# Dealing MLP groups out by TensorE's time, with their results worked on one phase later, in a fused attention and gMLP kernel

## The chip, the cores and the metric

The kernel runs on one core of a Trainium2 chip, alone. The metric is the time of one execution on the device in microseconds (us); a kernel is judged by the median of several runs. The five engines of the core work through instruction streams of their own, each in program order: TensorE (PE in the profile) does matrix products into PSUM, VectorE (DVE), ScalarE (ACT) and GpSimd (POOL) do elementwise work, and SyncE (SP) issues most DMAs.

## The reference

Eight batches of block-causal attention (8 heads, 576 positions, 64 columns a head), whose output, with the heads side by side, goes through a gated MLP with a mixing product along the positions:

```python
scores = scale * np.matmul(q, k.transpose(0, 1, 3, 2))
scores = np.where(block_i >= block_j, scores, -1000000000.0)      # blocks of 64
attn = softmax(scores)                                             # max, exp, sum
x = np.matmul(attn, v)            # -> (8, 576, 512), heads side by side
h = np.maximum(x @ w_in, 0.0)                                      # 512 -> 1024
u, v = h[..., :512], h[..., 512:]
v_n = (v - mu) / np.sqrt(var + 1e-06)                              # over the 512 columns
v_s = np.einsum('ts,bsd->btd', w_spatial, v_n) + b_spatial[None, :, None]
return (u * v_s) @ w_out                                           # 512 -> 512
```

## The kernel before

All of it is one program that Python writes out step by step; a pool of tiles and semaphores adds the waits, and `own(...)` keeps every instruction at the place on its engine at which it was written. So the order of the Python loop is the order of each engine's stream.

**Steps.** The heads are taken two at a time: 8 batches of 4 pairs, 32 pairs, and a pair is seven steps (`NS = 7`), one for each of the `SLOTS` into which its softmax is cut. Slot 0 is the last 64 queries of both heads, slots 1 and 2 the first 256 queries of the two heads, slots 3 and 4 the next 128, slots 5 and 6 the last 128. At step 0 of a pair TensorE gets the score products of slots 0, 1 and 2 (`scores_last`, L295, and `scores`, L283), at step 3 (`RUN2`) those of slots 3 to 6 and, behind them, the product of the probabilities with v (`av`, L464 and L481) of an earlier pair. Step i runs `exps` of slot i: VectorE subtracts the mask and finds the maximum (L318, L327), ScalarE takes the exponential with its sum (L334). `norm`, one step later, has VectorE invert the sums (L345, L348) and GpSimd multiply (L352). Then the probabilities are transposed, by VectorE and a DMA through the tile `turned` (L408, `move` L422), or in the first batch and the last pair by TensorE (L380).

**Split operands.** From the second batch on, products are made of two parts, a rounded `hi` and the rest `lo`, with three products for one. Each pair's q and k are split by `prep_pair`, which starts at step 4 of the pair before: ScalarE copies both halves of `raw` to `hi` (L244), then GpSimd subtracts four slices into `lo` (L247), two of them written at step 4 and two at step 5. There is one `hi` and one `lo` tile: `hi` can be rewritten only when the current pair's score products of step 3 are done, and the next pair's `scores_last` at step 0 needs the last slice of `lo` in its third product.

**MLP groups.** When a batch's four pairs are through, `moe(b)` makes a queue of 29 groups of matmuls, each into one of four PSUM banks (`ps_m`, shared with `av`): 5 `v_group` (V below; L512, and L522 for the short fifth one), 8 `u_group` (U, L606), 8 `sp_group` (S, L630 to L635) and 8 `out_group` (O, L664). They are dealt out over the 28 steps of the next batch: each step adds `rate` (groups by steps) to `credit`, and one group is written for each whole credit, whatever it takes. A group's result is worked on later: `later(k, phase, f)` has f written k steps on, in that step's phase. `due(0)` comes first in a step, before the scores and the exponentials; `due(1)` behind `exps` and `norm`; `due(2)` and `due(3)` at the end, behind the groups. Of a group written in step n, the first work on its result (ScalarE's relu or copy, L530, L615, L672; VectorE's gate, L639) is written in phase 0 of step n+1, so ahead of the exponentials of that step.

**The first batch.** Its pairs use `raw` as it is and have no groups beside them; the weights are loaded and split meanwhile and during the second batch (`spread(weights, ...)`), on VectorE, ScalarE and GpSimd.

## Time and profile before

| | us |
|---|---|
| runs of the kernel before | 791.61, 807.21, 800.57 (median 800.57) |
| the profiled execution, its time | 797.51 |
| its span, first to last instruction | 795.7 |
| first batch, without split operands | 4.80 to 56.77 |
| pairs beside which weights are still prepared | 56.77 to 203.10 |
| five like batches and one pair more | 203.10 to 683.25 |
| last pair and what is left of the MLP | 683.25 to 795.7 |

The profile is that of one execution. A row of the chain of waits gives a start, a duration and the piece of work; a row of the timeline gives the same and, in square brackets, how long the engine had stood idle before it and what released it. A row of the table of stretches gives the length of a stretch, the busy time of the five engine columns with their numbers of instructions, TensorE's granted clock as a share of full speed, and the share and rate of the DMA engines. PEld is TensorE's weight loading, which runs beside the products. Times count from the span's start. The boundaries of the table above are starts of `scores_last` of a pair.

### The profile page before, as it was taken

The page shows a single profiled execution, that of the slowest core. Times are in us where ns is not written, and L with a number is a line of the kernel's source. Part 1 is how long each engine was busy: PE and PEld are TensorE (multiplying, and loading weights), DVE is VectorE, ACT ScalarE, POOL GpSimd, SP SyncE. Part 2 cuts the span into 40 slices and gives each one's busy share as a digit, 9 for nine tenths or more (in the row PEclk, how much of TensorE's full clock was granted, in tenths as well). Part 3 has the DMA queues.
Part 4 walks back from the last instruction along what each step waited for, and adds up shares of the span by engine and source line. Part 5 has one row for each costly group of instructions (what it writes and reads, how often), then busy time and mean ns, then how long its engine had stood idle before and what let it go on. Part 6 is the DMA issues. An engine that isn't in the chain of part 4 may idle for free.

```text
span 795.7 us, 16364 instructions
## 1 busy us (share of the span) xinstructions
PE 715.7 (90%) x5729; PEld 635.5 (80%) x5729; DVE 465.2 (58%) x1587; ACT 426.4 (54%) x1156; POOL 342.6 (43%) x529
## 2 busy tenths in 40 slices
PE   8876968898988898998988899988988989899998
PEld 5554757787888787887878788887878988799898
DVE  5657877754774557745684557745675456731430
ACT  5775574443663457634763457634664437642542
POOL 4557467642444543344434543355344434341011
PEclk9997877989998999999998999999989889899999
DMA  7322445334444454345444354444544344431001
GB/s 259 123 72 93 128 126 157 88 116 136 124 116 130 127 157 112 105 123 146 130 130 130 101 165 115 113 115 139 152 129 102 97 121 132 98 99 36 26 1 60
DMA packets 42150, 92.05 MB, mean 116 GB/s; under 512 B 9298, under 2 KB 18002, under 8 KB 42068
## 3 DMA queue, kind: packets, MB, share of 16 engines
q1 hardware_dynamic: 32852, 81.56, 37.8%
q10 hardware_dynamic: 9216, 9.44, 3.5%
q8 instruction: 45, 0.74, 0.4%
q14 instruction: 37, 0.30, 0.1%
HBM read 38.18 MB, written 9.44 MB: 60 GB/s over the span
## 4 chain that ended last, share of the span: by engine, by line
PE 66%; POOL 13%; DVE 9%; issue 5%; ACT 4%; DMA 2%; SPq 1%; POOLq 0%; DVEq 0%; ACTq 0%
PE mo L664 10%; PE ms L630 10%; PE mu L606 10%; PE s L283 9%; PE mv L512 9%; POOL lo L247 7%; PE avh L464 6%; POOL p L352 4%; PE s L295 3%; PE avl L464 3%; DVE p L318 2%; PE avh L481 2%; DVE q L408 2%; ACT p L334 1%; PE t L380 1%
## 5 line engine op out<-in xcount | busy, mean ns | idle before, releaser
L334 ACT ACTIVATE p<-p,nmax 128x384 f32<-128x384 f32 (+4 forms) x288 | 167.3, 582 | 207.0 <-DVE nmax L318 97.0
L352 POOL TENSOR_SCALAR p<-p,ssum 128x384 f32<-128x384 f32 (+4 forms) x288 | 161.5, 575 | 197.9 <-DVE ssum L348 166.0
L247 POOL TENSOR_TENSOR lo<-raw,hi 128x288 fp32r<-128x288 f32 x112 | 95.3, 872 | 110.4 <-issue 89.0
L318 DVE CUSTOM_DVE_ANT_0 p<-s,mask 128x128 f32<-128x128 f32 (+3 forms) x256 | 117.3, 481 | 21.0 <-PE t L380 13.9
L606 PE MATMUL mu<-x,wi_hi 128*128 128x288 f32 x512 | 119.9, 316 | 0.0
L408 DVE STREAM_TRANSPOSE q<-p 128x384 f32<-128x384 f32 (+1 forms) x189 | 108.6, 612 | 16.7 <-POOL p L352 8.2
L649 POOL TENSOR_TENSOR gl<-u,gh 128x288 fp32r<-128x288 f32 x64 | 51.7, 809 | 110.5 <-ACT gh L648 110.5
L639 DVE TENSOR_TENSOR u<-ms,u 128x288 f32<-128x288 f32 x64 | 29.2, 456 | 116.2 <-PE ms L635 116.2
L606 PEld LDWEIGHTS mu<-x,wi_hi 128*128 128x128 f32 x512 | 91.9, 204 | 3.7 <-issue 0.9
L512 PE MATMUL mv<-wi_hi,x 128*128 128x512 f32 x256 | 84.5, 397 | 0.0
L630 PE MATMUL ms<-ws_hi,vh 128*128 128x288 f32 x256 | 82.7, 323 | 0.2 <-ACT q L386 0.2
L630 PE MATMUL ms<-ws_lo,vh 128*128 128x288 f32 x256 | 79.6, 311 | 0.0
L630 PE MATMUL ms<-ws_hi,vl 128*128 128x288 f32 x256 | 79.6, 311 | 0.0
L664 PE MATMUL mo<-gh,wo_hi 128*128 128x288 f32 x256 | 77.8, 304 | 0.0
L664 PE MATMUL mo<-gl,wo_hi 128*128 128x288 f32 x256 | 76.8, 300 | 0.0
L664 PE MATMUL mo<-gh,wo_lo 128*128 128x288 f32 x256 | 76.7, 299 | 0.0
L295 PE MATMUL s<-hi,lo 128*128 128x288 f32 x56 | 22.3, 399 | 59.4 <-POOL lo L247 59.4
L606 PE MATMUL mu<-x,wi_lo 128*128 128x288 f32 x256 | 75.4, 314 | 0.0
L295 PEld LDWEIGHTS s<-hi,lo 128*128 128x128 f32 x56 | 12.7, 227 | 64.5 <-POOL lo L247 64.5
L512 PEld LDWEIGHTS mv<-wi_hi,x 128*128 128x128 f32 x256 | 48.4, 189 | 10.8 <-issue 0.6
L630 PEld LDWEIGHTS ms<-ws_hi,vh 128*128 128x128 f32 x256 | 52.4, 205 | 3.0 <-issue 1.3
L334 ACT ACTIVATION_READ_ACCUMULATOR p<-p,nmax 128x1 f32 x288 | 54.3, 189 | 0.0
(118 smaller groups left out, 1620.7 us busy)
## 6 DMA issues: line engine op xcount, KB each, us to landing
turned<-q SPq DMA_DIRECT2D x216, 100.0 KB, 2.2
turned<-q SPq DMA_DIRECT2D x216, 96.0 KB, 2.2
raw<-qk SPq DMA_DIRECT2D x31, 608.0 KB, 4.1
v<-v SPq DMA_DIRECT2D x32, 320.0 KB, 4.3
outT<-o ACTq DMA_DIRECT2D x64, 144.0 KB, 1.8
rwi<-w_in SPq DMA_DIRECT2D x8, 512.0 KB, 4.3
rwo<-w_out SPq DMA_DIRECT2D x4, 512.0 KB, 4.4
rws<-w_spT SPq DMA_DIRECT2D x4, 288.0 KB, 3.1
```

Of the source, the lines that this page charges most:

```text
L247: own(nc.gpsimd.tensor_tensor(out=lo[:, cs], in0=raw[:, cs], in1=hi[:, cs].bitcast(F32), op=ALU.subtract))
L283: own(nc.tensor.matmul(banks[(b, pr, i + hd)][:, o:o + n], a[js, qs], k[js, :n], start=(m == 0), stop=(m == len(parts) - 1),))
L295: own(nc.tensor.matmul(bk[z][:, :HT], a[:, Q8:], k[:, z * HT:(z + 1) * HT], start=(m == 0), stop=(m == len(parts) - 1),))
L318: own(nc.vector.tensor_tensor_reduce(out=pt[:, o:o + n], in0=bk[:, o:o + n], in1=mask[:, 512 - n:], scale=-0.125, scalar=BIG, op0=ALU.add, ...
L334: own(nc.scalar.activation(pt[:, o:o + n], pt[:, o:o + n], AF.Exp, bias=mx, scale=-1.0, accum_out=ssum[:, s0 + r:s0 + r + 1],))
L352: own(nc.gpsimd.tensor_scalar(out=pt[:, o:o + w], in0=pt[:, o:o + w], scalar1=ssum[:, r:r + 1], scalar2=1.0, op0=ALU.mult, op1=ALU.mult,))
L408: own(nc.vector.transpose(to[:, :, o:o + 32 * n].rearrange("p r (c j) -> p c r j", j=32), pt[:, :n * P].rearrange("p (c r j) -> p c r j", ...
L464: own(nc.tensor.matmul(out[js, (t0 - q0) * P:(t1 + 1 - q0) * P].rearrange("p (t a j) -> p a t j", a=4, j=32), vt[:, c, js], src[:, :, o:o ...
L512: own(nc.tensor.matmul(ps, xs[k][:, j, cs], w[:, k, DH:], start=(n == 0), stop=(n == 3 * NC - 1),))
L606: own(nc.tensor.matmul(ps[:, :HT], w[:, k, ds], xs[k][:, j, zs], start=(n == 0), stop=(n == 3 * NC - 1),))
L630: own(nc.tensor.matmul(ps[:, :HT], a[:, ds], w[:, k, zs], start=(n == 0), stop=False))
L664: own(nc.tensor.matmul(ps[:, :HT], w[:, k, es], a[:, k, :], start=(n == 0), stop=(n == 3 * ND - 1),))
```

## The change

Three things are changed.

The queue of groups carries with each group a length in us of TensorE's time (V 2.75, U 1.6, S 1.85, O 1.6), and `PAIR_LENGTHS` has that of the score products of step 0 (1.8), of those of step 3 (1.45) and of `av` (2.95). A step adds `pace`, the batch's whole length over its steps, to `owed`; the score products and `av` take their length off it; groups are written while `owed` is above 0. So the steps with score products get few groups or none and the others get more. In the queue the U group that stood between the fourth and the fifth V group moves behind the fifth.

What is done with a group's result moves from phase 0 to phase 1 of the next step, behind that step's exponentials: the copies, relus and gates. What stood in phase 1 (the rest of x, L443, and the gate's splitting, L648 and L649) moves to phase 2; the tail copy of x (L489) and `begin(b)` move a step on, and the rest of the V groups (L582) moves ahead of the groups of its step.

In the first batch `av` and TensorE's transposes come a step sooner, and the second batch's first pair, the first with split operands, is split from step 2 to step 5 of the pair before it instead of steps 4 and 5.

```diff
-AV_AT, BOOT_AV = 2 * NS + RUN2, NS + 5
+AV_AT, BOOT_AV = 2 * NS + RUN2, NS + 4
+
+PAIR_LENGTHS = (1.8, 1.45, 2.95)
@@ x_evac, av
-        later(1, 0, hi)
-        later(1, 1, lo)
+        later(1, 1, hi)
+        later(1, 2, lo)
...
-        later(1, 2, lambda: own(nc.gpsimd.tensor_scalar(
+        later(2, 1, lambda: own(nc.gpsimd.tensor_scalar(
@@ v_group
-            later(1, 0, evac)
+            later(1, 1, evac)
             later(1, 2, stats)
             later(2, 1, scale)
             later(2, 2, normal)
-            later(3, 2, rest)
+            later(3, 1, rest)
@@ u_group, sp_group, out_group
-            later(1, 0, evac)
+            later(1, 1, evac)
...
-            later(1, 0, gate)
-            later(1, 1, split_g)
+            later(1, 1, gate)
+            later(1, 2, split_g)
...
-            later(1, 0, leave)
+            later(1, 1, leave)
@@ the queue
-        def groups(f, need, *args):
-            return [(need, lambda a=a: f(*a)) for a in args]
+        def groups(f, length, need, *args):
+            return [(need, lambda a=a: f(*a), length) for a in args]
...
-        order = "vvuvuvuvuuuuu" if b else "v" * 5 + "u" * 8
+        order = "vvuvuvvuuuuuu" if b else "v" * 5 + "u" * 8
@@ begin
-        rate = len(queue) / steps if b < B - 1 else 1.0
+        pace = (sum(q[2] for q in queue) + sum(PAIR_LENGTHS) * steps / NS) / steps
@@ the loop over steps
-            if i == RUN2 + 1 and b > 0:
-                spread(prep_pair(b, pr), 6, n, n + 2)
+            if i == (2 if boot else RUN2 + 1) and b > 0:
+                spread(prep_pair(b, pr), 6, n, n + (4 if boot else 2))
...
-                    later(1, 3, lambda b=b: begin(b))
+                    later(2, 1, lambda b=b: begin(b))
...
-        if at(n - 4) and by_pe(at(n - 4)[:2]):
-            for j in TURNS[(i - 4) % NS]:
-                transposes_pe(*at(n - 4)[:2], j)
-        credit = min(credit + rate, 2.0)
-        while credit >= 1.0 and queue and queue[0][0]():
-            queue.pop(0)[1]()
-            credit -= 1.0
+        if at(n - 3) and by_pe(at(n - 3)[:2]):
+            for j in TURNS[(i - 3) % NS]:
+                transposes_pe(*at(n - 3)[:2], j)
+        if here and not boot and i in (0, RUN2):
+            owed -= PAIR_LENGTHS[0] if i == 0 else PAIR_LENGTHS[1]
+        if i == RUN2 and NPAIR + 1 < g < len(pairs):
+            owed -= PAIR_LENGTHS[2]
+        owed = min(owed + pace, 3.0)
+        while owed > 0.0 and queue and queue[0][0]():
+            _, group, length = queue.pop(0)
+            group()
+            owed -= length
```

The first place to look at is TensorE in the fifth batch's first pair (its number is 4, its pair 0; an S group is `ms`, numbered by batch, half and column block). Before, the S group `ms_2_1_1` follows `av`:

```order
L464 MATMUL avl_3_2_4276<-turned_122,v_3_2_3968 64x128 x2
L464 MATMUL avh_3_2_4277<-turned_122,v_3_2_3968 64x128 x14
L481 MATMUL avh_3_2_4277<-turned_122,v_3_2_3968 64x64 x10
L630 MATMUL ms_2_1_1_4324<-ws_hi_114,vh_2_0_3598 128x288
L630 MATMUL ms_2_1_1_4324<-ws_lo_115,vh_2_0_3598 128x288
L630 MATMUL ms_2_1_1_4324<-ws_hi_114,vl_2_0_3599 128x288
```

After the change it ends ahead of the score products of step 3, here those of slots 3 and 4:

```order
L636 MATMUL ms_2_1_1_4251<-ws_a_116,vs_a_118 128x288
L637 MATMUL ms_2_1_1_4251<-ws_b_117,vs_b_119 128x288
L285 MATMUL s_4_0_3_4272<-hi_4_0_4046 128x384
L285 MATMUL s_4_0_4_4273<-hi_4_0_4046 128x384
L285 MATMUL s_4_0_3_4272<-lo_4_0_4047,hi_4_0_4046 128x384
L285 MATMUL s_4_0_4_4273<-lo_4_0_4047,hi_4_0_4046 128x384
```

No group is left at this step. The groups behind `av` and ahead of the next pair's `scores_last` are, for the four kinds of pair from the one with the fourth V group on, V U V' U before and V V' U after; U S S S both times; S O S O before and O S O S after; O O O V V before and O V V after (V' is the short fifth V group).

VectorE's stream at that place keeps its rows: before,

```order
L318 ISA p_4_0_3_4321,nmax_4_0_3_4319<-s_4_0_3_4260,mask_93 128x384
L318 ISA nmax_4_0_3_4319 128x1
L639 TENSOR_TENSOR u_2_3606<-ms_2_1_1_4324,u_2_3606 128x288
L318 ISA p_4_0_4_4348,nmax_4_0_4_4347<-s_4_0_4_4261,mask_93 128x384
L318 ISA nmax_4_0_4_4347 128x1
L443 TENSOR_TENSOR x_3_2_4339<-avl_3_2_4276,x_3_2_4339 128x256
```

and after,

```order
L320 ISA p_4_0_3_4333,nmax_4_0_3_4331<-s_4_0_3_4272,mask_93 128x384
L320 ISA nmax_4_0_3_4331 128x1
L641 TENSOR_TENSOR u_2_3648<-ms_2_1_1_4251,u_2_3648 128x288
L320 ISA p_4_0_4_4347,nmax_4_0_4_4346<-s_4_0_4_4273,mask_93 128x384
L320 ISA nmax_4_0_4_4346 128x1
L445 TENSOR_TENSOR x_3_2_4350<-avl_3_2_4288,x_3_2_4350 128x256
```

The gate of `ms_2_1_1` still stands between the maxima of slots 3 and 4, but the group that it waits for now stands ahead of `av` on TensorE instead of behind it.

The third place is ScalarE in the same batch's pair 2, from the exponential of slot 3 to the copies to `hi`. Before, the relu of the fourth V group (`mv_3_3`) stands ahead of the exponential of slot 4:

```order
L334 ACTIVATE p_4_2_3_4925,ssum_4_2_3_4924<-p_4_2_3_4925,nmax_4_2_3_4923 128x384
L566 ACTIVATE vr_3_2_4814<-vr_3_2_4814,st_3_2_4815 128x512
L574 CAST vh_3_2_4947<-vr_3_2_4814 128x512
L439 CAST x_4_0_4950<-avl_4_0_4880 128x256
L439 CAST x_4_0_4950<-avh_4_0_4881 128x320
L530 ACTIVATE vr_3_3_4932<-mv_3_3_4931 128x512
L334 ACTIVATE p_4_2_4_4960,ssum_4_2_3_4924<-p_4_2_4_4960,nmax_4_2_4_4959 128x384
L244 CAST hi_4_3_4965<-raw_4_3_4736 128x576
L244 CAST hi_4_3_4965<-raw_4_3_4736 128x640
```

and after:

```order
L336 ACTIVATE p_4_2_3_4924,ssum_4_2_3_4923<-p_4_2_3_4924,nmax_4_2_3_4922 128x384
L617 ACTIVATE u_3_4840<-mu_3_0_1_4843 128x288
L568 ACTIVATE vr_3_2_4813<-vr_3_2_4813,st_3_2_4814 128x512
L576 CAST vh_3_2_4932<-vr_3_2_4813 128x512
L336 ACTIVATE p_4_2_4_4940,ssum_4_2_3_4923<-p_4_2_4_4940,nmax_4_2_4_4939 128x384
L441 CAST x_4_0_4944<-avl_4_0_4879 128x256
L441 CAST x_4_0_4944<-avh_4_0_4880 128x320
L246 CAST hi_4_3_4948<-raw_4_3_4736 128x576
L246 CAST hi_4_3_4948<-raw_4_3_4736 128x640
```

The relu of the fourth V group has gone behind the copies to `hi`, and the relu of a U group has come in behind the exponential of slot 3.

More of the change, by code (lines that the diff above doesn't have):

```diff
@@ L673, in leave @@
                 nc.scalar.dma_start(outT[b, es, z * HT:(z + 1) * HT], o)
-            later(1, 0, leave)
-        def groups(f, need, *args):
-            return [(need, lambda a=a: f(*a)) for a in args]
+            later(1, 1, leave)
+        def groups(f, length, need, *args):
+            return [(need, lambda a=a: f(*a), length) for a in args]
         def free():
             return True
-        vs = groups(v_group, free, *((c,) for c in range(FULL + 1)))
-        us = groups(u_group, free, *((z, d) for z in range(2) for d in range(ND)))
-        sps = [groups(sp_group, lambda: ready["v"] > FULL, *((z, d) for d in range(ND)))
+        vs = groups(v_group, 2.75, free, *((c,) for c in range(FULL + 1)))
+        us = groups(u_group, 1.6, free, *((z, d) for z in range(2) for d in range(ND)))
+        sps = [groups(sp_group, 1.85, lambda: ready["v"] > FULL, *((z, d) for d in range(ND)))
                for z in range(2)]
-        outs = [groups(out_group, lambda z=z: ready[z] == ND, *((z, e) for e in range(NO)))
+        outs = [groups(out_group, 1.6, lambda z=z: ready[z] == ND, *((z, e) for e in range(NO)))
                 for z in range(2)]
-        order = "vvuvuvuvuuuuu" if b else "v" * 5 + "u" * 8
+        order = "vvuvuvvuuuuuu" if b else "v" * 5 + "u" * 8
         queue = [(vs if w == "v" else us).pop(0) for w in order]
@@ L751 @@
     queue = []
-    rate = 0.0
-    credit = 0.0
+    pace = 0.0
+    owed = 0.0
     TURNS = ((0,), (), (1, 2), (), (3, 4), (), (5, 6))
@@ L767, in begin @@
     def begin(b):
-        nonlocal rate
+        nonlocal pace
         queue.extend(moe(b))
         steps = NPAIR * NS + (0 if b else AV_AT - BOOT_AV)
-        rate = len(queue) / steps if b < B - 1 else 1.0
+        pace = (sum(q[2] for q in queue) + sum(PAIR_LENGTHS) * steps / NS) / steps
     n = -1
```

## The prediction

> **What bounds the kernel now.** I read the page first, then TensorE's waits, the table of stretches, and the timeline around one wait.
>
> ```profile
> span 795.7 us, 16364 instructions
> ...
> PEclk9997877989998999999998999999989889899999
> ...
> PE 66%; POOL 13%; DVE 9%; issue 5%; ACT 4%; DMA 2%; SPq 1%; POOLq 0%; DVEq 0%; ACTq 0%
> ```
> ```profile
> PE s L295 <- POOL lo L247: 61.5, 26, 4.8
> ```
>
> TensorE is the bound, but the chain leaves it for a quarter of the span, through GpSimd and VectorE, and its clock is below full in most of the 40 slices. One wait dominates: 61.5 us in 26 waits of `scores_last` for the last slice of `lo`. Next the stretches: five batches, cut where the pair with the fourth V group starts, and one pair more; then the stages with weights and at the end.
>
> ```profile
> 203.10:295.45 92.35, 84.71 (x706) 76.61 (x705) 56.84 (x198) 50.12 (x138) 40.72 (x65) 0.94 0.47 126
> 295.45:384.51 89.06, 81.72 (x705) 73.97 (x704) 56.35 (x198) 50.12 (x138) 40.06 (x64) 0.98 0.47 127
> 384.51:476.35 91.84, 84.48 (x705) 76.61 (x704) 56.38 (x198) 50.13 (x138) 40.09 (x64) 0.94 0.47 128
> 476.35:567.10 90.75, 83.23 (x706) 75.43 (x704) 56.13 (x198) 50.00 (x138) 40.07 (x64) 0.96 0.46 125
> 567.10:663.16 96.06, 88.72 (x705) 80.45 (x704) 56.77 (x198) 50.34 (x138) 40.06 (x64) 0.89 0.45 122
> 663.16:683.25 20.09, 20.09 (x167) 17.64 (x166) 16.40 (x61) 14.85 (x39) 6.02 (x11) 1.00 0.42 115
> ```
> ```profile
> 56.77:203.10 146.33, 118.40 (x862) 102.53 (x860) 99.39 (x306) 77.75 (x209) 85.36 (x113) 0.85 0.45 122
> ...
> 683.25:795.70 112.45, 106.60 (x841) 101.03 (x839) 34.83 (x105) 45.73 (x113) 22.85 (x35) 0.97 0.17 48
> ```
>
> A batch takes 92.0 us on average (460.06 over five), with some 7 us of TensorE idle and 0.89 to 0.98 of the clock. The clock is the second loss: behind a wait TensorE often runs at half clock, as here behind the waits that ended at 407.43 and 429.90 us.
>
> ```profile
> 409.20:412.60 3.40, 3.40 (x15) 3.40 (x16) 2.98 (x17) 1.90 (x4) 1.36 (x2) 0.51 0.69 241
> ...
> 430.00:436.60 6.60, 6.60 (x32) 6.10 (x33) 1.09 (x5) 1.19 (x3) 2.73 (x4) 0.50 0.54 173
> ```
>
> Why is `lo` late? The timeline of a pair of the S O S O kind:
>
> ```profile
> 349.19 0.40 PE L283 MATMUL s<-hi,lo 64*128 64x512 f32 x2
> ...
> 352.57 0.43 ACT L439 CAST x<-avh 128x320 fp32r<-128x320 f32 x1 [1.24 <-PE avh L481]
> ...
> 354.60 0.46 DVE L639 TENSOR_TENSOR u<-ms,u 128x288 f32<-128x288 f32 x1 [4.33 <-PE ms L635]
> ...
> 355.63 0.62 ACT L334 ACTIVATE p<-p,nmax 128x384 f32<-128x384 f32 x1 [2.63 <-DVE nmax L318]
> ...
> 356.57 1.30 ACT L244 CAST hi<-raw 128x576 fp32r<-128x576 f32 x2
> ...
> 358.00 1.58 POOL L247 TENSOR_TENSOR lo<-raw,hi 128x288 fp32r<-128x288 f32 x2 [0.44 <-ACT hi L244]
> ...
> 359.55 0.30 POOL L489 TENSOR_SCALAR xs<-x 128x128 fp32r<-128x128 f32 x1
> ...
> 359.83 1.15 POOL L352 TENSOR_SCALAR p<-p,ssum 128x384 f32<-128x384 f32 x2
> ...
> 360.94 1.67 POOL L247 TENSOR_TENSOR lo<-raw,hi 128x288 fp32r<-128x288 f32 x2
> ...
> 362.66 0.40 PE L295 MATMUL s<-hi,lo 128*128 128x288 f32 x1 [2.63 <-POOL lo L247]
> ```
>
> The scores of step 3 end at 349.59 and `av` at 352.55 (2.98). Then TensorE runs an S group, whose gate stands on VectorE ahead of slot 4's maximum: VectorE is idle 4.33 us, ScalarE 2.63 behind it, and `hi`, `lo`, the multiplications and the last `lo` follow in line until 362.61. The whole softmax chain starts when the group behind `av` has ended, 5 us after its scores were there.
>
> **The change part by part.** It adds no instruction. *The groups' results behind the exponentials, and no group at step 3.* Nothing on VectorE or ScalarE now waits for a group behind `av` before `hi` is copied; `av` itself still stands ahead, for x's copies come before `hi`. So from `av`'s end: copy of x 0.43, `hi` 1.30, `lo` 1.58, multiplications 1.15, xs 0.30, `lo` 1.67, sum 6.43 us. What covers it are the groups behind `av` and two products of `scores_last` that need no late `lo` (0.27). Their durations:
>
> ```profile
> 344.71 1.59 PE ms L630 x12
> ...
> 346.57 1.60 PE mo L664 x12
> ...
> 388.13 2.76 PE mv L512 x12
> ...
> 390.89 1.58 PE mu L606 x12
> 392.46 1.42 PE s L283 x12
> ```
>
> S is 1.86 with its two last products, O 1.60, V 2.76, U 1.58, V' 1.9 (8 of V's 12 products). Behind `av` stand after the change U S S S = 7.2, S and O twice = 6.9, O V V = 7.1: more than 6.16 (6.43 less 0.27), by 0.7 to 1.0. These three waits should go, if no engine arrives late. V V' U = 6.2 would just do, but there ScalarE and VectorE are full. Its rows before:
>
> ```profile
> 395.65 0.62 ACT L334 ACTIVATE p<-p,nmax 128x384 f32<-128x384 f32 x1 [1.22 <-POOL p L352]
> 396.27 0.82 ACT L566 ACTIVATE vr<-vr,st 128x512 f32<-128x512 f32 x1
> 397.12 0.62 ACT L574 CAST vh<-vr 128x512 fp32r<-128x512 f32 x1
> ...
> 399.80 0.60 ACT L530 ACTIVATE vr<-mv 128x512 f32<-128x512 f32 x1 [1.45 <-PE mv L512]
> 400.29 0.61 ACT L334 ACTIVATE p<-p,nmax 128x384 f32<-128x384 f32 x1
> 400.89 1.29 ACT L244 CAST hi<-raw 128x576 fp32r<-128x576 f32 x2
> ...
> 405.25 2.13 POOL L247 TENSOR_TENSOR lo<-raw,hi 128x288 fp32r<-128x288 f32 x2
> ...
> 407.43 0.40 PE L295 MATMUL s<-hi,lo 128*128 128x288 f32 x1 [2.40 <-POOL lo L247]
> ```
>
> The exponential of slot 3 starts at 395.65, late by itself. From there, after the change: it 0.62, a relu of U 0.4, 0.82 and 0.55 for the V group, slot 4's 0.61, x 0.35 and 0.43, `hi` 1.29, so 400.7 instead of 402.2; then 1.58, 1.15, 0.30 and 1.7 make 405.5 instead of 407.4. TensorE, its scores done at 393.9, `av` 2.98, groups 6.2 and 0.27, is there at 403.3: a wait of 2.2 stays, for one U has left this pair.
>
> A batch by pairs: 384.51 to 405.5 is 20.7 from the third product of `scores_last` on. The others are TensorE's own work, `scores_last` to `scores` 1.7 and 1.42, `av` 2.98, and groups: U⁴+U S³ 19.5, S³O+S²O² 20.0, O⁴+O V² 19.6. Sum 79.8, and 1.3 for half clock, since one wait in four stays (a stretch of 3.4 us costs 1.7): 81.1 instead of 92.0. Five batches save 54.6, the pair more loses 0.6: **54**. Bounds: 0, if the chain does not shorten, and 70, if the batch is TensorE's own 77.5 at full clock.
>
> *The stage with weights*, 56.77 to 203.10: 27.9 idle (146.33 less 118.40) and 0.15 of the clock, 22. The sooner split works on the first wait:
>
> ```profile
> 60.23 2.12 POOL L247 TENSOR_TENSOR lo<-raw,hi 128x288 fp32r<-128x288 f32 x2
> ...
> 62.39 0.61 PE L295 MATMUL s<-hi,lo 128*128 128x288 f32 x1 [4.84 <-POOL lo L247]
> ```
>
> Three slices go ahead of the multiplications, one `lo` of about 1.0 is left behind, so I take 2.5 of its 4.84. Copies of weights stay in line on ScalarE and GpSimd, two pairs have no group or only V groups as cover. I take a third of both, **17**; bounds 0 and 46.
>
> *The end*, 683.25 on: one wait and one half-clock stretch, 5.9 idle and 0.03 of the clock, 3.4; **4**, bounds 0 and 8. The rest is TensorE back to back, and dealing by time cannot shorten it. *The first batch*, `av` and transposes a step sooner: TensorE's work in another order; 0, between -3 and 3, since each probability has one step less to be ready. *The queues of DMAs* are moved past nothing but ScalarE's own copies for `outT`, which go with their groups. *Banks*: with two groups in a step and the result copied one step later, four banks hold two steps; ScalarE's copy must be done while the next step's groups run, 2.8 us. No wait of TensorE for it shows before; 0, up to 1.5 us a pair.
>
> 797.5 less 54, 17 and 4 is 722.5, say **723 us**. The profiled execution is 0.4% below the median, which lies well inside the runs.
>
> [...] The trace has waits of 2.40 and 2.63 followed by 3.4 us at half clock or by none. [...]
>
> **The rivals.** *A new wait takes half back* (0.20): the margins are 0.7 to 1.0, and each `lo` may take 0.5 longer (2.13 against 1.67) as VectorE now works beside it; a bank or a late exponential does the same. 1.5 us at each of 28 pairs is 42: 765. For it: VectorE's 56.4 us of a batch would be 70% of 81. Against: no other wait of a size before. *Everything goes* (0.08): the V pair's wait too, and the clock stays full: 723 less 5 times 3.6, less 5 in the weights, 700. *Slower* (0.07): the chain stays as long as it was, because `av` and x's copies ahead of `hi`, not the gate, hold it. Then the shorter covers decide: 1.6 less in the V pair, 3.2 less behind O O O V V, which loses its shelter. With a chain c from `av`'s end the four waits of a batch are 4c less 28.5 (the covers with 0.27 each); that exceeds some 8 us of waits before (three of 2.4 to 2.7) once c is above 9.1, and before c was 10.06 (352.55 to 362.61). 4.8 a batch is 25 in 5.25 batches, with half clock about 30: 828. Against it: the 4.33 us that VectorE stood idle for a gate. *No change* (0.05): shorter chain and shorter cover cancel, 798.
>
> **How the numbers follow.** The forecast has 0.60, with 708 to 742 as its own range. 2% of 800.6 is 16, about what a measurement tells from no change. Faster than 784.6: 0.60, 0.20 and 0.08 less a little for rivals that run past it, 0.86; within, 0.06; slower, 0.08. The range of 8 in 10 is 700 to 772.
>
> **What would show it.** In the profile after: TensorE's wait for `lo` down from 61.5 to below 25 us; VectorE's idle ahead of a gate no longer ahead of slot 4's maximum; the batches at 80 to 83 us with the clock at 0.97 or more; the V pair still with a wait of about 2. Wrong it is if a wait for ScalarE or VectorE (a bank, `hi`) appears ahead of TensorE's groups, or if the waits before `scores_last` keep their 2.6 us in the S and O pairs.

## The result, and the profile after

| | before | after |
|---|---|---|
| runs, median us (lowest to highest) | 796.43 (791.61 to 807.21), 4 runs | 742.66 (740.65 to 745.81), 4 runs |
| ratio, 95% interval | | 0.935 (0.926 to 0.943) |
| profiled execution, its time and span | 797.51, 795.7 | 742.46, 740.7 |

The forecast was 723, with 700 to 772 as the range of 8 in 10 and 708 to 742 as the forecast's own. The time fell by 6.5%, 20 us less than forecast, and lies just outside the narrower range. The ratios, here and below, leave out those executions of the kernel before that took over 1.5% more than its fastest, so they are not the quotients of the medians. Lines of functions behind the new table stand 2 lower in the changed kernel, so `scores_last` is L297 and the `lo` of `prep_pair` is L249.

The page of the changed kernel, as it was read before: span, granted clock in 40 slices, chain by engine.

```profile
span 740.7 us, 16338 instructions
...
PEclk9997888999999999999989999999989999999999
...
PE 53%; DVE 11%; issue 11%; POOL 10%; ACT 9%; DMA 4%; SPq 2%; ACTq 1%; DVEq 0%; POOLq 0%
```

Of the clock's 40 digits six are now below 9, where eleven were. TensorE's waits (engine, what waits, released by what: us, times, longest):

```profile
PE s L297 <- POOL lo L249: 40.3, 25, 4.6
```

The wait for the last slice of `lo` fell from 61.5 to 40.3, where below 25 had been forecast. The table of stretches, by stages cut at the same places of the program as before (starts of `scores_last`): the stage with weights, the five like batches, the pair more, the end.

```profile
50.11:182.40 132.29, 109.54 (x861) 95.65 (x860) 100.90 (x308) 77.53 (x208) 85.75 (x110) 0.90 0.48 134
...
182.40:267.32 84.92, 81.25 (x705) 73.75 (x704) 57.76 (x199) 50.28 (x139) 40.40 (x65) 0.98 0.50 135
267.32:352.00 84.68, 81.11 (x706) 73.82 (x705) 56.94 (x198) 50.12 (x138) 40.08 (x64) 0.98 0.49 134
...
522.73:608.36 85.63, 82.06 (x705) 74.59 (x704) 57.66 (x198) 50.19 (x138) 40.16 (x64) 0.96 0.50 135
608.36:626.83 18.47, 18.47 (x155) 16.05 (x154) 14.24 (x53) 13.37 (x35) 5.02 (x9) 1.00 0.50 135
...
626.83:740.70 113.87, 106.85 (x853) 101.52 (x851) 36.91 (x112) 46.89 (x117) 23.80 (x37) 0.99 0.17 49
```

Where the 55.0 us of span come from, from these rows and those shown before:

| stage | before | after | saved | forecast |
|---|---|---|---|---|
| up to the second batch's start | 56.77 | 50.11 | 6.7 | 0 (-3 to 3) |
| with weights | 146.33 | 132.29 | 14.0 | 17 |
| five batches | 460.06 | 425.96 | 34.1 | 54.6 |
| the pair more | 20.09 | 18.47 | 1.6 | -0.6 |
| the end | 112.45 | 113.87 | -1.4 | 4 |

A batch takes 85.2 us, not 81.1. Of the 34.1 us that five batches saved, 19.1 are idle time of TensorE (37.2 less 18.1) and 15.0 busy time (422.86 less 407.84), most of which half clock had stretched (51.2 us of it before, 23.9 after). Now the timeline of a pair of the S O S O kind, the one that the prediction read for the cause:

```profile
321.60 0.56 DVE L320 CUSTOM_DVE_ANT_0 p<-s,mask 128x384 f32<-128x384 f32 x1 [1.89 <-PE s L285]
...
322.09 0.45 DVE L641 TENSOR_TENSOR u<-ms,u 128x288 f32<-128x288 f32 x1
322.46 0.55 DVE L320 CUSTOM_DVE_ANT_0 p<-s,mask 128x384 f32<-128x384 f32 x1
...
325.25 0.43 ACT L441 CAST x<-avh 128x320 fp32r<-128x320 f32 x1 [0.29 <-PE avh L483]
325.57 1.30 ACT L246 CAST hi<-raw 128x576 fp32r<-128x576 f32 x2
...
329.96 1.72 POOL L249 TENSOR_TENSOR lo<-raw,hi 128x288 fp32r<-128x288 f32 x2
...
332.42 0.30 PE L297 MATMUL s<-hi,lo 128*128 128x288 f32 x1
```

The gate (L641) is ready when VectorE gets there, slot 4's maximum follows at once, and ScalarE waits only for `av` itself. `lo` is there at 331.68, before TensorE asks for it. So here the step did what was forecast. The pair with the fourth V group is where it did not:

```profile
270.53 0.69 DVE L544 BATCH_NORM_STATS2 st<-vr 128x6 f32<-128x512 f32 x1 [0.79 <-ACT vr L532]
...
276.31 0.58 ACT L532 ACTIVATE vr<-mv 128x512 f32<-128x512 f32 x1
...
276.92 0.70 DVE L544 BATCH_NORM_STATS2 st<-vr 128x6 f32<-128x512 f32 x1 [0.86 <-ACT vr L532]
...
279.29 0.53 DVE L320 CUSTOM_DVE_ANT_0 p<-s,mask 128x384 f32<-128x384 f32 x1
...
279.92 0.62 ACT L336 ACTIVATE p<-p,nmax 128x384 f32<-128x384 f32 x1 [1.52 <-POOL p L354]
...
283.37 1.31 ACT L246 CAST hi<-raw 128x576 fp32r<-128x576 f32 x2
...
284.81 1.58 POOL L249 TENSOR_TENSOR lo<-raw,hi 128x288 fp32r<-128x288 f32 x2 [3.64 <-issue]
286.36 1.15 POOL L354 TENSOR_SCALAR p<-p,ssum 128x384 f32<-128x384 f32 x2
286.44 0.40 PE L297 MATMUL s<-lo,hi 128*128 128x288 f32 x1 [0.36 <-POOL lo L249]
...
287.74 1.68 POOL L249 TENSOR_TENSOR lo<-raw,hi 128x288 fp32r<-128x288 f32 x2
...
289.48 0.40 PE L297 MATMUL s<-hi,lo 128*128 128x288 f32 x1 [2.65 <-POOL lo L249]
```
```profile
291.20:294.60 3.40, 3.40 (x15) 3.40 (x16) 3.19 (x11) 1.25 (x4) 1.37 (x2) 0.50 0.72 269
```

The pair starts at 267.32, so slot 3's exponential comes 12.6 us behind its start (before: 395.65 less 384.51, 11.1). The reason stands in the first three rows: a V group's relu (L532) is now behind the exponentials on ScalarE, and VectorE, which takes its work in order, stands at `bn_stats` (L544) until the relu is done, 0.79 us at one V group of the pair and 0.86 at the next. All that is behind it on VectorE, slot 3's maximum too, comes later. TensorE waits 0.36 and 2.65 us, and a stretch at half clock follows.

One more row that the prediction had not counted is in the next pair, with U S S S behind `av`:

```profile
305.04 0.37 ACT L441 CAST x<-avl 128x256 fp32r<-128x256 f32 x1 [2.30 <-PE mu L608]
...
310.02 1.71 POOL L249 TENSOR_TENSOR lo<-raw,hi 128x288 fp32r<-128x288 f32 x2
...
311.79 0.40 PE L297 MATMUL s<-hi,lo 128*128 128x288 f32 x1 [0.57 <-POOL lo L249]
```

`av` ended at 303.61, but the copy of x started at 305.04, when the U group behind `av` was done. That group is the last of its batch, and x has five buffers for four pairs: the reading of the code is that the copy needs the buffer which this group still reads.

### The profile page after: what moved, and what is told of

It reads as the page before. It is cut to its first block, busy times and chain, and to the rows that moved or that the text cites. A ratio compares the mean times of both kernels' runs of the same rounds, so it can differ in the third digit from the quotient of the medians.

```text
span 740.7 us, 16338 instructions
## 1 busy us (share of the span) xinstructions
PE 686.9 (93%) x5729; PEld 614.2 (83%) x5729; DVE 472.2 (64%) x1587; ACT 425.5 (57%) x1156; POOL 344.3 (46%) x529
## 4 chain that ended last, share of the span: by engine, by line
PE 53%; DVE 11%; issue 11%; POOL 10%; ACT 9%; DMA 4%; SPq 2%; ACTq 1%; DVEq 0%; POOLq 0%
PE mo L666 10%; PE mu L608 10%; PE ms L632 10%; PE s L285 7%; POOL lo L249 5%; ACT p L336 4%; PE mv L514 4%; POOL p L354 4%; PE avh L466 3%; PE s L297 3%; DVE q L410 2%; PE avl L466 2%; DVE p L320 2%; DVE st L544 2%; PE t L382 2%
## 5 line engine op out<-in xcount | busy, mean ns | idle before, releaser
L336 ACT ACTIVATE p<-p,nmax 128x384 f32<-128x384 f32 (+4 forms) x288 | 167.4, 582 | 183.9 <-DVE nmax L329 82.3
L354 POOL TENSOR_SCALAR p<-p,ssum 128x384 f32<-128x384 f32 (+4 forms) x288 | 165.8, 590 | 185.1 <-DVE ssum L350 149.6
L249 POOL TENSOR_TENSOR lo<-raw,hi 128x288 fp32r<-128x288 f32 x112 | 94.3, 863 | 85.5 <-issue 67.2
L320 DVE CUSTOM_DVE_ANT_0 p<-s,mask 128x128 f32<-128x128 f32 (+3 forms) x256 | 117.3, 481 | 16.8 <-PE s L285 13.4
L632 PE MATMUL ms<-ws_hi,vh 128*128 128x288 f32 x256 | 76.2, 298 | 0.0
L632 PE MATMUL ms<-ws_hi,vl 128*128 128x288 f32 x256 | 75.3, 294 | 0.0
L632 PE MATMUL ms<-ws_lo,vh 128*128 128x288 f32 x256 | 75.3, 294 | 0.0
L641 DVE TENSOR_TENSOR u<-ms,u 128x288 f32<-128x288 f32 x64 | 29.0, 453 | 48.2 <-PE ms L637 47.9
L608 PEld LDWEIGHTS mu<-x,wi_lo 128*128 128x128 f32 x256 | 53.3, 208 | 0.6
L297 PE MATMUL s<-hi,lo 128*128 128x288 f32 x56 | 20.2, 361 | 35.2 <-POOL lo L249 35.2
L445 DVE TENSOR_TENSOR x<-avl,x 128x256 fp32r<-128x256 f32 x32 | 13.5, 423 | 60.3 <-ACT x L441 60.3
```

The costliest lines, as they stand in the source:

```text
L249: own(nc.gpsimd.tensor_tensor(out=lo[:, cs], in0=raw[:, cs], in1=hi[:, cs].bitcast(F32), op=ALU.subtract))
L297: own(nc.tensor.matmul(bk[z][:, :HT], a[:, Q8:], k[:, z * HT:(z + 1) * HT], start=(m == 0), stop=(m == len(parts) - 1),))
L320: own(nc.vector.tensor_tensor_reduce(out=pt[:, o:o + n], in0=bk[:, o:o + n], in1=mask[:, 512 - n:], scale=-0.125, scalar=BIG, op0=ALU.add, ...
L336: own(nc.scalar.activation(pt[:, o:o + n], pt[:, o:o + n], AF.Exp, bias=mx, scale=-1.0, accum_out=ssum[:, s0 + r:s0 + r + 1],))
L354: own(nc.gpsimd.tensor_scalar(out=pt[:, o:o + w], in0=pt[:, o:o + w], scalar1=ssum[:, r:r + 1], scalar2=1.0, op0=ALU.mult, op1=ALU.mult,))
L608: own(nc.tensor.matmul(ps[:, :HT], w[:, k, ds], xs[k][:, j, zs], start=(n == 0), stop=(n == 3 * NC - 1),))
```

## The experiments

Theory at the start: of the batch's loss, nearly all is the V pair's wait and the half clock behind it, and its cause is the place of the V groups' relu. Rivals: the two halves of the change (phases and dealing) do not add up because of something else, such as x's copies or the order of `lo` and the multiplications. All times below are medians of four executions; "before" was 803.65 us in the first four, 801.35 in the next four, 800.63 in the last three. A batch is a fifth of the five like batches, and the clock that of this stretch.

| kernel | us | ratio (95%) | a batch | clock | TensorE's wait for `lo` in five batches | second batch starts |
|---|---|---|---|---|---|---|
| before | 796 to 804 | 1 | 92.0 | 0.94 | 37.2 | 56.77 |
| after | 742.66 | 0.935 (0.926 to 0.943) | 85.2 | 0.97 | 18.1 | 50.11 |
| phases alone | 760.89 | 0.956 (0.947 to 0.966) | 85.7 | 0.99 | 23.3 | 63.02 |
| dealing alone | 751.46 | 0.943 (0.931 to 0.956) | 85.1 | 0.96 | 13.3 | 58.66 |
| after, first batch as before | 752.18 | 0.946 (0.936 to 0.956) | 84.7 | 0.97 | 15.0 | 63.05 |
| after, V relu first | 720.65 | 0.905 (0.896 to 0.915) | 81.5 | 1.00 | 10.2 | 50.50 |
| after, V statistics later | 731.16 | 0.913 (0.908 to 0.918) | 82.3 | 1.00 | 9.6 | 48.98 |
| after, `lo` first | 729.30 | 0.915 (0.909 to 0.921) | 83.2 | 0.97 | 8.3 | 48.54 |
| after, V relu and `lo` first | 707.39 | 0.889 (0.883 to 0.895) | 79.7 | 1.00 | 0 | 50.55 |
| the same, `hi` first too | 716.30 | 0.900 (0.893 to 0.907) | 81.4 | 1.00 | 0 | 47.77 |
| after, late split | 743.28 | 0.933 (0.927 to 0.939) | 85.2 | 0.97 | 18.1 | 48.36 |
| first batch as before, x too | 748.52 | 0.936 (0.931 to 0.941) | 84.9 | 0.97 | 15.7 | 60.27 |
| V relu and `lo` first, x as before | 707.60 | 0.884 (0.879 to 0.890) | 79.9 | 1.00 | 0.6 | 49.85 |

**The halves alone.** In the first, only the phases change and groups are dealt by their number:

```diff
 # the kernel before
-        later(1, 0, hi)
-        later(1, 1, lo)
+        later(1, 1, hi)
+        later(1, 2, lo)
...
-            later(1, 0, evac)
+            later(1, 1, evac)
...
-                    later(1, 3, lambda b=b: begin(b))
+                    later(2, 1, lambda b=b: begin(b))
```

> Only the phases are changed: results of groups one phase later, dealing by count and the first batch as before. Theory (the chain to lo is freed because nothing in front of the copies to hi waits for a group): a group still stands behind av at step 3, and its copy or relu, though behind the exponential of slot 4, still stands ahead of hi. So the chain from av's end keeps that group's 1.6 to 2.8 us, 8 to 9.5 us against covers of 6.9 to 7.8: waits of 1 to 2 at three pairs of four, time 760 to 775. Rival (the dealing by time brings all of it): no change, 788 to 800.

In the second, only the dealing and the order of the queue change, with the phases and the first batch of before.

```diff
 # the changed kernel
-        later(1, 1, hi)
-        later(1, 2, lo)
+        later(1, 0, hi)
+        later(1, 1, lo)
...
-            later(1, 1, evac)
+            later(1, 0, evac)
...
-AV_AT, BOOT_AV = 2 * NS + RUN2, NS + 4
+AV_AT, BOOT_AV = 2 * NS + RUN2, NS + 5
```

> Only the dealing by time and the queue's order are changed: results are worked on in phase 0 as before, and the first batch is as before. Theory: with no group at step 3 there is no result to wait for at step 4, so the chain to hi is freed without the phases; what stays is that the gates and relus of the other steps stand ahead of the maxima, 1 to 2 us in the pairs with V groups: 750 to 765. Rival of the prediction (the chain keeps its length, av holds it): covers shorter by 1.6 and 3.2 us make it slower than before, 800 to 830. Second rival (dealing is all): 742 to 750.

Both times, 760.89 and 751.46, lie at the lower end of what their theories said, and two rivals fell: the phases alone do not leave the time as it was, and shorter cover does not make it slower. The third, that dealing is all (742 to 750), is not refuted. The dealing alone takes 748.68 to 756.53, and the kernel with both halves and the same first batch, which follows below, 752.18: on top of the dealing the phases bring nothing that these times can tell from zero, since what they gain later they lose in the first batch. In the five batches too a batch takes 85.7 with the one, 85.1 with the other, and 85.2 with both. The halves do not add up: the second finds a loss that the first has already taken, and what is left, the V pair's wait, neither cures. With the phases alone TensorE stands idle there for 2.70 us (3.21 in one batch), with the dealing alone for 2.27 (1.54 in one), with both for 3.0 (0.36 and 2.65).

**The first batch.** The changed kernel without its parts there (`BOOT_AV`, the transposes' step, the sooner split):

```diff
 # the changed kernel
-AV_AT, BOOT_AV = 2 * NS + RUN2, NS + 4
+AV_AT, BOOT_AV = 2 * NS + RUN2, NS + 5
...
-            if i == (2 if boot else RUN2 + 1) and b > 0:
-                spread(prep_pair(b, pr), 6, n, n + (4 if boot else 2))
+            if i == RUN2 + 1 and b > 0:
+                spread(prep_pair(b, pr), 6, n, n + 2)
...
-        if at(n - 3) and by_pe(at(n - 3)[:2]):
+        if at(n - 4) and by_pe(at(n - 4)[:2]):
...
```

> The changed kernel without its parts in the first batch: av and transposes by TensorE a step later again, the first split pair split at steps 4 and 5 again. Theory (these parts bring the 6.7 us by which the second batch starts sooner, 50.1 against 56.8): 748 to 752, with the second batch's start at 55 to 57. Rival (the first batch gained from something else, or gives its gain back in the stage with weights): 740 to 745.

The time, 752.18, is at the upper end of what the theory said, but not for the reason given: the second batch starts at 63.05, later than the 56.77 of the kernel before, not sooner. Phases alone have it at 63.02. So the phases make the first batch longer, by 4 to 5 us in its last two pairs (18.39 and 20.33 with the phases alone, 14.73 and 23.11 here, 13.91 and 19.73 before), and the parts for the first batch take 13 off again. The start of the second batch changes by some 2 us for other reasons too: with the dealing alone it is at 58.66, with the first batch's streams as before. The rows of the third pair, before and with the phases alone:

```profile
23.13:37.04 13.91, 12.43 (x103) 7.92 (x102) 8.78 (x35) 9.85 (x30) 7.36 (x12) 1.00 0.34 109
```
```profile
24.30:42.69 18.39, 16.02 (x104) 10.29 (x102) 9.74 (x38) 10.66 (x32) 7.84 (x13) 0.76 0.33 107
```
```profile
32.98 2.06 PE L283 MATMUL s<-raw 64*128 64x384 f32 x4 [1.41 <-DVE nmax L327]
```

TensorE waits 1.41 us there for a maximum (before, 0.19), and over the pair its clock is 0.76 of full speed; a stretch of 10.2 us at half clock begins in it, at 33.72. To see whether x's copies do this, their phases alone were put back in the first batch:

```diff
 # the changed kernel without its parts in the first batch
-        later(1, 1, hi)
-        later(1, 2, lo)
+        later(1, 1 if b else 0, hi)
+        later(1, 2 if b else 1, lo)
```

> The changed kernel without its parts in the first batch, and with the copies of x in the first batch also in their old phases (0 and 1). Theory (the phases make the first batch some 6 us longer, 63.05 for the second batch's start in place of 56.77, because x's copies there go behind the exponentials and hold the banks and the maxima): the second batch starts at 56 to 58 us, the time is 745 to 748. Rival (the length comes from something else, such as the weights' background work): it starts at 62 to 64, 750 to 754.

The two pairs beside which x is copied are back at 14.02 and 19.73 us (before 13.91 and 19.73; without the edit 14.73 and 23.11), and the wait at that place is 0.19 again. The second batch starts at 60.27, between the two forecasts, since the first two pairs took 3 us more than before in this execution (second pair 13.57 against 11.29, with 4.6 us at half clock, of which 2.3 were lost, by an estimate from the granted share of 0.5); what brought the half clock there was not settled. The time, 748.52, too lies between the two. It is 3.7 below that without the edit, but the two intervals overlap, so that the times do not show this difference; the lengths of the pairs do.

Which part of the edit for the first batch brings the gain:

```diff
 # the changed kernel
-            if i == (2 if boot else RUN2 + 1) and b > 0:
-                spread(prep_pair(b, pr), 6, n, n + (4 if boot else 2))
+            if i == RUN2 + 1 and b > 0:
+                spread(prep_pair(b, pr), 6, n, n + 2)
```

> The changed kernel with the first split pair split at steps 4 and 5 again, as before; av and the transposes of the first batch stay a step sooner. Theory (the first batch's gain comes from av and the transposes, the sooner split is worth little): the second batch still starts at about 50 us, its wait for lo grows from 4.2 to 4.7 us; 742 to 745. Rival (the sooner split brings the first batch's gain): the second batch starts at 55 us or later, 748 to 752.

743.28, the same as the changed kernel. In the second batch's first pair TensorE's idle time up to the third product grew from 3.86 to 5.67 us (1.21 and 4.46), and the pair began 1.75 sooner. So `av` and the transposes bring the gain, and the sooner split is worth nothing that can be measured.

**The V groups' relu.** One line, in `v_group` alone:

```diff
 # the changed kernel
-            later(1, 1, evac)
+            later(1, 0, evac)
             later(1, 2, stats)
```

> The changed kernel with the relu of the V groups alone back in phase 0, ahead of the exponentials. Theory (in the pair with V groups the relu behind the exponential holds VectorE's statistics, and with it slot 3's exponential, which stands 12.6 us behind the pair's start against 11.1 before): the exponential of slot 3 comes 1 to 1.5 us sooner, the wait of 3.0 at the next pair falls to 1.5 to 2, with less half clock: 732 to 738. Rival (ScalarE and VectorE are full there whatever the order): 741 to 745, the wait still 2.7 to 3.1.

720.65, better than its theory: the batch 81.5. The rows of the V pair that starts at 263.63, and the stretch of the five batches:

```profile
271.83 0.68 DVE L544 BATCH_NORM_STATS2 st<-vr 128x6 f32<-128x512 f32 x1
...
274.82 0.62 ACT L336 ACTIVATE p<-p,nmax 128x384 f32<-128x384 f32 x1 [1.52 <-POOL p L354]
...
284.39 0.40 PE L297 MATMUL s<-hi,lo 128*128 128x288 f32 x1 [1.44 <-POOL lo L249]
```
```profile
182.17:589.65 407.48, 397.29 (x3522) 361.23 (x3520) 287.74 (x986) 250.68 (x690) 200.75 (x321) 1.00 0.52 141
```

`bn_stats` no longer waits, slot 3's exponential comes 11.2 us behind the pair's start instead of 12.6, the wait is 1.4 instead of 3.0, and no stretch at half clock is left in the five batches (1.00). The like wait right behind them, of 1.43 us, was followed by 3.4 us of it, so that the clean five are in part luck (the last section has more). The expectation had counted the wait and only part of the clock.

Whether it is VectorE's waiting in line or the relu's place on ScalarE was tried in the other direction: the relu stays behind the exponentials, and VectorE's part moves one step on.

```diff
 # the changed kernel, with bufs=3 instead of 2 for vr
             later(1, 1, evac)
-            later(1, 2, stats)
-            later(2, 1, scale)
-            later(2, 2, normal)
-            later(3, 1, rest)
+            later(2, 1, stats)
+            later(3, 1, scale)
+            later(3, 2, normal)
+            later(4, 1, rest)
```

> The changed kernel with the relu of a V group left behind the exponential, as the change has it, but what VectorE does with that relu (bn_stats and all behind it) written one step later, so that VectorE no longer stands waiting for ScalarE's relu; a third buffer for vr holds the groups that are then under way. Theory (the V pair is late because VectorE waits in line for the relu): exponential of slot 3 some 11.2 us behind the pair's start as with the relu first, where the changed kernel has 12.6; the V pair's wait at 1.6 or less; 718 to 728. Rival (the place of the relu on ScalarE itself is what costs): the exponential of slot 3 stays at 12.6 and the time at 738 to 746.

```profile
271.36 0.69 DVE L544 BATCH_NORM_STATS2 st<-vr 128x6 f32<-128x512 f32 x1
...
279.93 0.62 ACT L336 ACTIVATE p<-p,nmax 128x384 f32<-128x384 f32 x1 [0.22 <-POOL p L354]
...
289.77 0.40 PE L297 MATMUL s<-hi,lo 128*128 128x288 f32 x1 [1.16 <-POOL lo L249]
```

The exponential comes 11.1 us behind the start (279.93 less 268.83), the wait falls to 1.2 (1.5 in one batch) and the half clock goes: the cause is VectorE's place in line. The third buffer for `vr` came with this edit and was not tried alone. The time, 731.16, is 3 above the forecast range: V's results are ready a step later, TensorE gets waits that it did not have, 3.7 us in the five batches for a bank that U's relu has not yet left, ahead of a product of `av`, and the five batches start later (186.69 against 182.40).

**What else stands in the line to `lo`.** All four slices of `lo` at step 4, ahead of the multiplications on GpSimd:

```diff
 # the changed kernel
-                spread(prep_pair(b, pr), 6, n, n + (4 if boot else 2))
+                spread(prep_pair(b, pr), 6, n, n + (4 if boot else 1))
```

> The changed kernel, with all four slices of the next pair's lo written at step 4 of a pair, ahead of the multiplications of slot 3's and 4's probabilities on GpSimd, instead of two at step 4 and two at step 5 behind them. Theory (what is left of the wait is the line copy of x, hi, lo, multiplications, lo): the multiplications (1.15 us) and xs (0.30) leave that line, so the V pair's wait falls from about 3.0 to about 1.5 us and that of the S and O pair from 0.7 to 0; behind waits of 1.5 no half clock follows; 720 to 726. Rival (the wait is set by the late copies to hi alone, or the later multiplications make the transposes and so av late): the time stays at 738 to 745, with a new wait ahead of av.

729.30, short of the forecast 720 to 726. The waits fell as said: 8.3 us in five batches, 1.5 in most V pairs (0.28 and 1.24), none in the S and O pairs. What did not follow was the clock. TensorE's rows at the V pair's end, and the stretch behind:

```profile
282.43 0.40 PE L297 MATMUL s<-lo,hi 128*128 128x288 f32 x1 [0.28 <-POOL lo L249]
284.07 0.40 PE L297 MATMUL s<-hi,lo 128*128 128x288 f32 x1 [1.24 <-POOL lo L249]
```
```profile
285.70:289.10 3.40, 3.40 (x16) 3.40 (x15) 3.23 (x11) 1.44 (x4) 0.15 (x1) 0.50 0.82 245
```

Half clock followed in each of the five batches, where behind the 1.44 with the V relu first it had followed in none. With both edits, `later(1, 0, evac)` in `v_group` and `n + 1` for the slices:

> The changed kernel with both edits: the relu of a V group ahead of the exponentials again, and all four slices of lo at step 4 ahead of the multiplications. Theory: the V pair's wait (1.6 with the first edit alone) falls to about 0.3, the S and O pair's to 0, batches of 79 to 80 us; 708 to 716. Rival (later multiplications bring a new wait ahead of av or of the groups): 718 or more, with TensorE's waits for turned or for av's operands in the place of those for lo.

707.39, the fastest time measured here; its interval, 0.883 to 0.895, lies clear of the changed kernel's 0.926 to 0.943. The five batches:

```profile
181.26:579.83 398.57, 397.72 (x3522) 361.48 (x3521) 286.51 (x986) 249.40 (x690) 201.07 (x320) 1.00 0.53 145
```

TensorE is busy 397.72 of 398.57 us at full clock, and in these batches it waits for `lo` no more. Taking the copies to `hi` forward too goes one step past the best:

```diff
 # the kernel with both edits
-            if i == (2 if boot else RUN2 + 1) and b > 0:
-                spread(prep_pair(b, pr), 6, n, n + (4 if boot else 1))
+            if boot and i == 2 and b > 0:
+                spread(prep_pair(b, pr), 6, n, n + 4)
...
+        if here and not boot and i == RUN2 + 1 and g + 1 < len(pairs):
+            split_next = prep_pair(*pairs[g + 1])
+            next(split_next)
+            spread(split_next, 5, n, n + 1)
         due(1)
```

> As the one before, with the copies to hi also written ahead of what step 4 does with the groups' results (copies of x, relus, gates), right behind slot 4's exponential. Theory: hi no longer waits for av, all waits for lo in the steady batches go, batches of 78 to 79 us; 700 to 711. Rival: the results of the groups are now worked on 1.3 us later on ScalarE, so that banks come free late and a wait of the groups for a bank takes the place of that for lo; 715 or more.

716.30, as the rival said. In the five batches TensorE's waits are now for a maximum and for a bank that U's relu has not yet left:

```profile
PE s L285 <- DVE nmax L320: 4.8, 10, 0.8
PE mu L608 <- ACT u L617: 2.7, 5, 0.5
```

Last, x's phases of before in the first batch (the edit of two lines shown above), in the best kernel:

> The changed kernel with the V groups' relu ahead of the exponentials, all four slices of lo ahead of the multiplications, and x's copies of the first batch in their old phases. Theory: if x's copies behind the exponentials cost 6 us in the first batch with av at its old step, they may cost some here; second batch's start at 45 to 50 us in place of 50.6, 702 to 707. Rival (with av a step sooner, nothing in the first batch waits for them any more): 707 to 709.

707.60, the same: with `av` a step sooner nothing there waits for x's copies any more.

Two things were not tried: the parts for the first batch alone, on the kernel before, and a sixth buffer for x. So that x's copy waits for its buffer remains a reading of the code and of one row, though the wait behind it (0.57) goes with `lo` first.

## Why the prediction was right, and where its sizes were off

**The gate ahead of slot 4's maximum holds the chain: right.** In the S O S O pair VectorE's 4.33 us and ScalarE's 2.63 are gone, and the waits behind S O S O and behind O V V with them. Either half of the change alone takes a batch from 92.0 to 85.1 or 85.7: it is enough that the gate stands elsewhere, or that its group ends sooner.

**The three waits go: two did, one nearly.** Behind U S S S 0.57 us stayed, because the line from `av`'s end was not 6.43 but 8.1 (303.61 to 311.73): the first 1.4 of it is x's copy waiting for the U group. The working started the line at `av`'s end because it does in the S O S O pair, and took that for all.

**The V pair's wait of 2.2: the mis-sized term.** It was 3.0 (0.36 and 2.65). From slot 3's exponential on, the line was as forecast (9.85 forecast, 9.5 measured: 279.92 to 289.42). What failed is the sentence ahead of it, that this exponential "starts at 395.65, late by itself. From there, after the change": the change itself moves that start by 1.5 us, through the V groups' relu and VectorE's `bn_stats`. The step followed the relus on ScalarE alone, and not who waits in line for them on another engine.

**1.3 us of half clock a batch: 2.4.** The five batches hold 23.9 us at half clock (0.50 in the row at 291.20), 4.8 a batch, half of it lost. With a wait of 3.0 every batch had a stretch; with 1.4 none of five had one, and the next pair did. The working had read the clock's row before as below full in most of the 40 slices; it shows it below 90% in 11. These two terms, 0.8 and 1.1, with the S and O pair's 21.36 (20.0 forecast, where the working's own durations give 20.2; 0.57 of the rest is the wait behind U S S S) are most of the 4.1 us a batch by which 81.1 was missed. With the relu ahead, the batch was 81.5.

**The stage with weights, 17: 14.0, near.** The sum is nearer than its parts: 5.2 us of idle time went and 8.9 of busy time, where a third of each, 9.3 and 7.3, was taken without a row for it. The 2.5 for the sooner split were worth nothing (742.66 against 743.28); a wait of 3.86 stays where it was to act.

**The first batch, 0 within 3: 6.7, outside.** Two effects that the term had taken for a mere reordering: the phases cost 4 to 5 there, `av` and the transposes a step sooner give 13. The bound was drawn from "one step less to be ready", and not from the rows of what TensorE waits for in that batch.

**The end, 4: -1.4.** One U group more (1.58) now lies in this stage, as one less lies in the pair more (18.47 instead of 20.09). At like work nothing changed there. The term took for gone a wait that is that of a V pair, and by the working's own account stays: 2.40 before, 0.36 and 2.64 after (at 627.49 and 630.53).

**Banks at nothing: right.** No wait for a bank shows in the five batches of the changed kernel. It appeared where ScalarE's copies went 1.3 us later still (0.5 a batch), and where V's statistics went a step on (0.75 a batch).

**What was luck.** The first batch gave 6.7 us where 0 was forecast, for reasons that the working did not have. Without it the time would be some 749. And two signs that were named failed: the wait for `lo` is 40.3 and not below 25, and the batches take 85.2 and not 80 to 83. The mechanism was right; the nearness of the sum is in part chance.

**The rivals.** A new wait that takes half back was the closest: a late exponential was named in it, and the size was half of what it priced (20.5 us less saved in the five batches, not 42). It came in one pair of four, not at every pair, and no `lo` grew slower beside VectorE: before, 5 of the 80 slices in the five batches took 1.38 us, each beside VectorE's subtraction for the rest of a V group (L582, 1.03 to 1.04 us), and the others at most 0.95; after, when that subtraction stands elsewhere, none of 80 took more than 0.97. That the chain is held by `av` and x's copies and the time rises, fell: in the S O S O pair the line from `av`'s end to the last `lo` is 6.5 us (325.18 to 331.68), where the rival needed 9.1. That everything goes (700) is what the best kernel nearly shows, 707.39, after two edits more.

**The clock behind a wait.** In the kernel before a wait of 2.40 us had 3.4 us of half clock behind it (407.43, 409.20) and one of 2.63 none (362.66). After, 3.0 us of waiting (0.36 and 2.65) had it behind them in each batch, and with `lo` first 1.5 us in all (0.28 and 1.24) had too: the length alone does not tell which.

## What to carry to other kernels

Where work on a result is moved behind other work of its engine, list who waits for that result on the other engines: an engine that takes its work in order passes the delay on to everything behind its wait (here VectorE's 0.79 and 0.86 us at `bn_stats` in one pair, and slot 3's exponential 1.5 us later). Whether the gains of two edits add up depends on whether they take the same wait: the two halves of this change did, and together they left a batch as long as either alone; the V groups' relu and `lo` first did not, and their 22.0 and 13.4 us make 35.4, against 35.3 measured together. And TensorE's waits were worth more here than their length: two edits of a line each, which took waits of 1 to 3 us away, are worth 35 us here (742.66 against 707.39). Of the 27.4 of it in the five batches 10.1 are busy time, which half clock had stretched (407.84 less 397.72).

## What the runs showed of the hardware

In the five batches the granted clock fell to half (0.50) in stretches of 3.4 us or twice that, and not by the wait's length alone. With the change, 0.36 to 0.47 and 2.64 or 2.65 us of waiting, with one product between, came with 3.4 or 6.8 us of it each time (in two batches it began before the wait had ended); with the dealing alone 2.27 with 6.8 in four batches, and 1.54 with 3.4 in the first; with the phases alone 2.70 with none in the first two batches and 3.4 in the last two, 3.21 with 3.4 in the third; 1.44 with the V relu first with none in five, and 1.43 with 3.4 in the pair behind them. But 0.28 and 1.24 of waiting, with `lo` first, came with 3.4 or 6.8 (in two of the five batches the 0.28 was 0.55 and 0.65).

Over the whole trace of the kernel before, its 19 stretches at half clock start on a grid of 3.41 us, to 0.01 us each, and so do the 11 in the span of the changed kernel. What goes with them is how long TensorE was busy in the 3.41 us ahead of a place of that grid. Three such pieces, each ending 0.2 us ahead of the place; the first is of the kernel with `lo` first and half clock followed it, the others are of the phases alone, hold a wait of 2.70 between them, and none followed (their places lie 79 and 80 steps of 3.41 us behind the half clock that began at 33.72):

```profile
282.09:285.50 3.41, 1.89 (x18) 1.45 (x17) 2.41 (x9) 2.09 (x6) 3.32 (x6) 1.00 0.67 158
```
```profile
299.76:303.17 3.41, 1.94 (x15) 1.70 (x13) 2.38 (x10) 2.49 (x6) 3.01 (x6) 1.00 0.69 161
303.17:306.58 3.41, 2.18 (x20) 1.88 (x21) 2.64 (x7) 1.25 (x4) 1.18 (x1) 1.00 0.58 141
```

TensorE was busy for 55% of the first, and for 57% and 64% of the others. In the trace of the changed kernel half clock followed those 11 of the pieces up to whose end the clock was full in which TensorE was busy least, for 0 to 52%, and none of the 186 others, which had 58% or more. In that of the kernel before it followed the 18 with 2 to 50%, and of the 181 others, which had 55% or more, one, with 58%. The 0.2 us were chosen to part them best, and no run was made to test it. So a wait of 1.5 us, within one piece, had half clock behind it where one of 2.70, across two, had none. A wait of 1.44 within one piece leaves 58% of it, by an estimate from the two lengths, and at 55 to 58% both were seen. Why half clock lasted one step of the grid or two was not settled.
